# A two-layer convolution and GeGLU kernel: convolution steps borrow a PSUM bank only when the plan has it empty, and the last row's second half gets a bank of its own

## The chip, the cores and the metric

The kernel runs on one core of a Trainium2 chip, as one program with one launch. The metric is the device time of that core in microseconds; smaller is better. Every figure below is a time of a run, a row of its profile, or worked out from such rows.

## The reference, cut to what matters

Two kinds of layer alternate, twice. The first multiplies the normalised input by a long convolution (as long as the sequence, 2048 rows of 576 columns) of `shift(k) * v`; the second is a gated feed-forward block with 4608 hidden columns. Both are added to the residual.

```python
def _A_ref(q, k, v, shift_k, ssm_k, ssm_D):
    kv = k_shift * v                     # k_shift: four-tap causal filter of k
    y = irfft(rfft(kv, 2*S) * rfft(ssm_k, 2*S))[:S] + kv * ssm_D
    return q * y
def _B_ref(x, w_gate, w_up, w_down):
    return (_gelu(x @ w_gate) * (x @ w_up)) @ w_down
x = A_q
x = x + _A_ref(_layernorm(x), ...); x = x + _B_ref(_layernorm(x), ...)
x = x + _A_ref(_layernorm(x), ...); x = x + _B_ref(_layernorm(x), ...)
```

The convolution does not depend on `x`, so it is computed once and used by both layers.

## The kernel before, in words

**Units, passes, visits.** The 2048 rows are four chunks of 512 rows. A unit is one layer's feed-forward block on one chunk; there are eight units (0 to 7), in the order layer 0 of chunks 0 and 1, layer 1 of chunks 0 and 1, and the same for chunks 2 and 3. The units are done in passes of one or two (0; 1, 2; 3, 4; 5, 6; 7), and each pass goes three times over a third of the hidden columns. That makes 24 visits, numbered 0 to 23 here. One visit is:

- twelve pairs `gu` (matmuls of line 889, 216 records in all): gate and up for 128 hidden columns; ScalarE applies the gelu (line 1412, or 1403 and 1404) and VectorE multiplies (line 1413 or 1405) into `hT`;
- four rows `dn` (line 1428): each row is 24 matmuls, 12 hidden tiles by two halves of 288 columns, accumulated in one PSUM tile. When a row is done VectorE adds it to the residual `x_c`, which is called the eviction here (lines 1449, 1462, 1468 or 1470, by visit).

**Convolution.** It is a transform in blocks. A forward step is four matmuls of 288 columns (line 288, tile `cps`; "F" below). ScalarE copies its result out of PSUM into `eo` (line 291, two buffers), and VectorE makes a sum and a difference of the two halves (line 296, two instructions, the crossing). An inverse step is eight matmuls (line 331, "INV"), copied out by ScalarE or VectorE. Products in between are VectorE's (lines 304 to 321, 482). Chunk 0's convolution is done before visit 0; those of the other chunks are worked into the visits.

**PSUM.** It is cut into four tiles of two 512-element fp32 banks each; the code calls each such tile a bank, and so does this text. Three of them go round among `gu` pairs, `dn` rows and borrowed convolution steps: `pr(name)` counts `taken` up and gives the next in turn. The fourth is the convolution's own.

**The planner.** One Python pass writes every engine's instructions in order, with a model clock `t` (`t.pe`, `t.dve`, `t.act`) and a cost for each kind of instruction. The order is then fixed: each engine runs its instructions in that order, and waits at semaphores where a tile is not ready. Between two hidden tiles of a row, `fill` puts in what the clock says is ready: late evictions (`run_late`), VectorE work of the convolution (`run_v`), and TensorE steps of the convolution (`run_p`, line 568 on).

`run_p` takes the own bank if `ps_free[0]` says that it is free, and otherwise borrows: it needs `ps_free[1]`, the time at which the last borrowed step was copied out, to be past, and `conv.alt` to be set. `conv.alt` is set once for each row (line 1423) and used up by one borrow, so that a row has one borrow at most. What the bank that comes next in turn still holds is not asked.

The eviction of a row is put into the queue `late` at the row's end with the number `taken[0]` (line 1473), and written into VectorE's order when the clock is 0.2 us past the row's end (`run_late`), or at the latest when `pr` is about to come round (line 633).

The last row of the last visit is done half by half (lines 1433 to 1440): twelve matmuls into half 0 of the row's tile, an add on VectorE (line 1438), a store, then twelve matmuls into half 1 of the same tile, an add and a store.

Of the kernel before, what the change touches and what calls it, by code (L numbers as in the profile page):

```python
# [27 lines left out]
NEVER = 1e9  # L28
# [7 lines left out]
C_TT, C_ST, C_BN, C_NORM, C_HT, C_GELU, C_EVA, C_EVD, C_YH = 0.76, 0.82, 0.47, 0.62, 0.69, 0.6, 0.66, 0.76, 0.8  # L36
# [7 lines left out]
class Pace:  # L44


    def __init__(self):
        self.pe = self.dve = self.act = 0.0
# [84 lines left out]
class Conv:  # L133
# [9 lines left out]
    def __init__(self, tc, ctx, pace, A_k, A_v, A_shift_k, A_ssm_k, A_ssm_D, ident, cps, ypool):  # L143
        self.tc, self.nc, self.t = tc, tc.nc, pace
        self.k2, self.v2, self.hk = A_k[0], A_v[0], A_ssm_k
        self.S, self.D = self.k2.shape
        self.NB = self.S // BS
        self.KS = A_shift_k.shape[1]
        self.sk, self.sD = A_shift_k, A_ssm_D
        self.ident, self.cps, self.ypool = ident, cps, ypool  # L150
        D = self.D
        pool = lambda name, bufs: ctx.enter_context(tc.tile_pool(name=name, bufs=bufs))
        self.cst = pool("c_cst", 1)
        self.krp = pool("c_kr", 3)
# [12 lines left out]
        self.V_ = self.cst.tile([P, 2, RT, P], BF16, name="V")  # L167
        self.nV = self.cst.tile([P, 3, P], BF16, name="nV")
        self.skc = self.cst.tile([P, self.KS, D], BF16, name="skc")
        self.y, self.yb = {}, {}  # L170
        self.kt_, self.vt_ = {}, {}
        self.y_at = {(0, j): 0.0 for j in range(RT)}
        self.z_at = {0: 0.0}
        self.kv_at, self.fwd_at, self.hf_at, self.hd_at = {}, {}, {}, {}
        self.ht = {}
        self.y_used = {}
        self.ps_free, self.cur, self.alt = [0.0, 0.0], 0, None
        self.neo = 0
        self.U = deque()
        self.kr_free, self.hr_free = [0.0] * 3, [0.0] * 4  # L180
        self.nkr = self.nhr = 0
        self.V, self.L, self.Pq = deque(), deque(), deque()
        self.left = 0
        self.spills = deque()
# [383 lines left out]
    def run_p(self):  # L568
        t = self.t
        if not self.Pq:  # L570
            return False
        ready, cost, run = self.Pq[0]
        self.cur = 0 if self.ps_free[0] <= t.pe else 1
        if ready() > t.pe or self.ps_free[self.cur] > t.pe or self.cur and self.alt is None:
            return False
        self.Pq.popleft()
        run()
        t.pe += cost
        return True

@with_exitstack
def ssm_geglu_kernel(ctx, tc, A_q, A_k, A_v, A_shift_k, A_ssm_k, A_ssm_D, B_x, B_w_gate, B_w_up,
# [23 lines left out]
    t = Pace()  # L606
# [10 lines left out]
    turn, taken = list(range(4)), [0]  # L617

    def bank(n, name, shape=(P, 2, 512), dt=F32):
        return banks[n].tile(list(shape), dt, tag="pr", name=name)  # L620

    late = deque()

    def run_late(limit):
        if not late or late[0][0] > t.pe or max(t.dve, t.pe - 1.0) + C_EVD > limit:
            return False
        ready, _, run = late.popleft()
        run()
        t.on_dve(C_EVD, ready)
        return True  # L630

    def pr(name):
        while late and taken[0] - late[0][1] >= 2:
            ready, _, run = late.popleft()
            run()
            t.on_dve(C_EVD, ready)
        taken[0] += 1
        return bank(turn[(taken[0] - 1) % 3], name)
    ypool = pool("y", 2)
    xpool = pool("x", 2)  # L640
# [9 lines left out]
    conv = Conv(tc, ctx, t, A_k, A_v, A_shift_k, A_ssm_k, A_ssm_D, ident,  # L650
                lambda *form: bank(turn[3], "cps", *form), ypool)
# [183 lines left out]
    def out_tile():  # L835
        if not xn_open():
            spreads(True)
            conv.flush(NEVER)
        return xn_tile()
# [52 lines left out]
    def gu_half(pair, fi, n):  # L892
        gu(pair, wgu[fi // FG], fi % FG, lambda a: a.rearrange("p (j q) -> p j q", q=P)[:, n::2, :], xnT_of[0])
# [3 lines left out]
    def turn_row(ui, j, xn, when, entry):  # L897
# [17 lines left out]
        conv.ps_free[0] = xn_at[ui]  # L915
        xn_done[ui] = j + 1

    early = {}
    due = []

    def when_due(when, load, n):
        due.append((when, len(due), load, n))
        due.sort(key=lambda d: d[0])
# [44 lines left out]
    with tc.manual_schedule():  # L968
# [385 lines left out]
        for at, (wb, ph, ui, first, final) in enumerate(visits):  # L1354
# [30 lines left out]
            free, gone = deque([0.0] * 3), deque([0.0] * 2, maxlen=2)  # L1385
            conv.alt = None
            for fi in range(FP):
                n, gi = divmod(wb * FP + fi, FG)
                w = wgu[n]
                if wb == 0 and fi in early:  # L1390
                    pair = early.pop(fi)
                    taken[0] += 1
                    gu_half(pair, fi, 1)
                    t.pe = max(t.pe, free.popleft()) + C_GU / 2
                else:
                    pair = pr("gu")
                    gu(pair, w, gi, lambda a: a, xnT)
                    t.pe = max(t.pe, free.popleft()) + C_GU
                while run_late(NEVER):
                    pass  # L1400
                if hurry() and t.act <= t.pe + 0.2:
                    ga = work.tile([P, 2, CH], BF16, tag="ga", name="ga")
                    nc.scalar.activation(out=ga[:, 0, :], in_=pair[:, 0, :], func=ACT.Gelu_apprx_tanh)  # L1403
                    nc.scalar.copy(out=ga[:, 1, :], in_=pair[:, 1, :])  # L1404
                    nc.vector.tensor_tensor(out=hT[:, fi, :], in0=ga[:, 0, :], in1=ga[:, 1, :], op=ALU.mult)  # L1405
                    there = t.on_act(2 * C_GELU, max(t.pe + 0.15, gone[0]))
                    gone.append(t.on_dve(C_HB, there + 0.15) + 0.1)
                    free.append(there + 0.1)
                    lead = FAR
                else:  # L1410
                    ga = work.tile([P, CH], F32, tag="ga", name="ga")
                    nc.scalar.activation(out=ga[:], in_=pair[:, 0, :], func=ACT.Gelu_apprx_tanh)  # L1412
                    nc.vector.tensor_tensor(out=hT[:, fi, :], in0=ga[:], in1=pair[:, 1, :], op=ALU.mult)  # L1413
                    gone.append(t.on_dve(C_HT, t.on_act(C_GELU, max(t.pe + 0.15, gone[0])) + 0.15) + 0.1)
                    free.append(gone[-1])
                    lead = LEAD
                if gi == FG - 1 and final:
                    when_due(t.pe + (FP - FG) * C_GU + 12.0, load_wgu, n + 3)
                fill(t.pe + C_GU + lead, hurry(), conv.left > 0)
            ahead[:] = [t.pe + RT * FP * C_DN, visits[at + 1][2] if at + 1 < len(visits) else None]  # L1420
            for j in range(RT):
                acc = pr("dn")
                conv.alt = lambda: pr("cps")
                xa = x_c[c][:, j, :]
                xh = xa.rearrange("p (h d) -> p h d", h=2)

                def down(fi, h):
                    nc.tensor.matmul(acc[:, h, 0:HW], lhsT=hT[:, fi, j * P:(j + 1) * P],  # L1428
                                     rhs=wd[2 * wb + fi // WT][:, fi % WT, h * HW:(h + 1) * HW],
                                     start=(fi == 0), stop=(fi == FP - 1))  # L1430
                if wb == NWB - 1 and j == RT - 1:
                    dst = out2[c * CH:(c + 1) * CH, :].rearrange("(p j) d -> p j d", j=RT)[:, j, :]
                    for h in range(2):
                        for fi in range(FP):
                            down(fi, h)
                        ob, entry = out_tile()
                        entry[0] = True
                        nc.vector.tensor_tensor(out=ob[:, 0:HW], in0=xh[:, h, :], in1=acc[:, h, 0:HW], op=ALU.add)  # L1438
                        nc.sync.dma_start(out=dst[:, h * HW:(h + 1) * HW], in_=ob[:, 0:HW])
                    break  # L1440
# [6 lines left out]
                if layer == 1 and end:  # L1447
# [6 lines left out]
                        entry[0] = True  # L1454
                    else:
                        conv.store(dst, ob, t.pe + 0.2 + C_EVD + LAG, entry)
                    t.on_dve(C_EVD, t.pe + 0.2)
                else:
                    def plus(c=c, j=j, layer=layer, ph=ph, end=end, acc=acc, xa=xa, xh=xh):
                        if end:  # L1460
# [64 lines left out]
```

## Time and profile before

| | |
|---|---|
| runs of the kernel before | 947.65, 948.48, 947.70 us; median 947.70 |
| profiled execution | 947.87 us, of which the span from first to last instruction is 946.1 us |
| granted TensorE clock | 0.999 |
| busy share of the span | TensorE 98%, VectorE 58%, ScalarE 35%, GpSimd 15% |

Each row of the profile's timeline gives the start, the duration, the engine, the line, the operation with its tiles, and how many instructions were merged; a bracket at the end gives the idle time of the engine just before, and whose signal ended it. Matmuls overlap their successors, so the bracket is a little shorter than the delay: the delay is the distance of two starts less what back-to-back matmuls need. The records of `dn`, F and INV start 0.122 to 0.123 us apart when nothing waits.

### The profile page before, as it was taken

How to read it: one execution, taken by the hardware profiler on the slowest of the kernel's cores; microseconds unless marked ns; L12 is line 12 of the kernel's file. 1: busy time of each engine (PE TensorE's matmuls, PEld its weight loads, DVE VectorE, ACT ScalarE, POOL GpSimd, SP SyncE). 2: the span in 40 equal slices, each digit the busy share in tenths (PEclk: the TensorE clock that was granted, in tenths of full speed). 3: DMA queues.
4: the chain of work that ended last, by engine and by line, in shares of the span. 5: the costliest groups of instructions: out<-in, count | busy, mean ns of one | idle time of the engine just before them, and what ended most of it. 6: DMA issues, size and time to landing. Idle time of an engine off the chain costs nothing.

```text
span 946.1 us, 19330 instructions
## 1 busy us (share of the span) xinstructions
PE 930.2 (98%) x8225; PEld 539.2 (57%) x8225; DVE 552.5 (58%) x1033; ACT 327.5 (35%) x591; POOL 137.5 (15%) x302
## 2 busy tenths in 40 slices
PE   8999999999999999999999999999999999999998
PEld 5756465564655646556556556456456456456555
DVE  7767676577989856767988533543333334433322
ACT  5665426542324235441222511551211214411211
POOL 3213101331114005221110200130000002100000
PEclk9999999999999999999999999999999999999999
DMA  9997999348825603963770730592540540696620
GB/s 241 270 239 194 262 239 179 114 109 200 242 66 168 143 24 100 231 184 88 174 240 15 139 88 20 96 202 38 113 114 1 117 110 8 122 223 151 146 68 26
DMA packets 125324, 130.14 MB, mean 138 GB/s; under 512 B 39731, under 2 KB 117428, under 8 KB 125237
## 3 DMA queue, kind: packets, MB, share of 16 engines
q1 hardware_dynamic: 115906, 92.46, 45.5%
q0 software_dynamic: 9200, 35.54, 11.9%
q8 instruction: 64, 1.05, 0.5%
q10 hardware_dynamic: 130, 0.90, 0.3%
q14 instruction: 24, 0.19, 0.1%
HBM read 108.53 MB, written 11.80 MB: 127 GB/s over the span
## 4 chain that ended last, share of the span: by engine, by line
PE 96%; DVE 2%; DMA 1%; ACT 1%; issue 0%; POOL 0%; SPq 0%; ACTq 0%; DVEq 0%
PE gu L889 59%; PE dn L1428 29%; PE cps L288 2%; PE ps L279 2%; PE cps L331 1%; PE ps L889 1%; DMA k<-in_A_k_dram 1%; PE ps L1092 1%; PE ps L1198 1%; PE ps L1124 0%; PE ps L1219 0%; DVE x_c L1468 0%; DMA xnT<-xn 0%; DVE kc L296 0%; DVE x_c L1462 0%
## 5 line engine op out<-in xcount | busy, mean ns | idle before, releaser
L889 PE MATMUL gu<-xnT,wgu 64*128 64x512 bf16 x5130 | 559.0, 377 | 0.6 <-DMA xnT<-xn 0.6
L889 PEld LDWEIGHTS <-wgu 64*128 64x128 bf16 x5238 | 254.9, 94 | 304.7 <-issue 8.5
L1412 ACT ACTIVATE ga<-gu 128x512 f32<-128x512 f32 x256 | 152.8, 597 | 473.7 <-PE gu L889 468.3
L1413 DVE TENSOR_TENSOR hT<-ga,gu 128x512 bf16<-128x512 f32 x256 | 175.9, 687 | 230.2 <-ACT ga L1412 229.0
L1428 PE MATMUL dn<-wd,hT 128*128 128x288 bf16 x2304 | 294.3, 286 | 0.5 <-DVE xn L1438 0.5
L1428 PEld LDWEIGHTS <-hT 128*128 128x128 bf16 x2304 | 223.4, 98 | 66.1 <-issue 10.1
L1470 DVE TENSOR_TENSOR x_c<-x_c,dn 128x576 f32<-128x576 f32 x32 | 24.1, 753 | 41.4 <-PE dn L1428 41.1
L721 POOL TENSOR_SCALAR means<-s 128x1 f32<-128x1 f32 x28 | 11.3, 403 | 211.1 <-DVE x_c L1462 164.6
L291 ACT ACTIVATE eo<-cps 128x576 f32<-128x576 f32 x48 | 30.9, 651 | 27.1 <-PE cps L288 13.7
L1468 DVE SCALAR_TENSOR_TENSOR x_c<-dn,means,x_c 128x576 f32<-128x576 f32 x28 | 22.9, 817 | 27.8 <-PE dn L1428 27.5
L737 POOL TENSOR_TENSOR rstd<-ve,neghalf_t 128x1 f32<-128x1 f32 x56 | 34.4, 615 | 4.7
L308 DVE TENSOR_TENSOR prod<-prod 128x576 bf16<-128x576 bf16 x72 | 33.0, 458 | 2.5
L1403 ACT ACTIVATE ga<-gu 128x512 bf16<-128x512 f32 x29 | 17.3, 597 | 43.9 <-PE gu L889 40.7
L397 POOL DMA_DIRECT2D kr<-Kd x24 | 13.2, 551 | 102.6 <-DVE prod L307 102.6
L401 POOL DMA_DIRECT2D hr<-Hd x36 | 19.5, 541 | 45.4 <-DVE prod L307 45.4
L1449 DVE TENSOR_TENSOR xn<-x_c,dn 128x576 bf16<-128x576 f32 x15 | 11.3, 755 | 23.8 <-PE dn L1428 23.8
L1405 DVE TENSOR_TENSOR hT<-ga 128x512 bf16<-128x512 bf16 x31 | 13.1, 422 | 19.2 <-ACT ga L1404 19.2
L729 ACT ACTIVATE junk<-x_c,nm 128x576 bf16<-128x576 f32 x28 | 21.5, 767 | 5.6 <-POOL nm L721 5.6
L721 POOL TENSOR_SCALAR nm<-s 128x1 f32<-128x1 f32 x28 | 7.9, 281 | 100.3 <-DVE x_c L773 100.3
L763 ACT ACTIVATE yh<-y,rstd 128x576 f32<-128x576 bf16 x28 | 21.4, 769 | 2.7 <-POOL rstd L737 2.7
L296 DVE TENSOR_TENSOR kc<-eo 128x288 bf16<-128x288 f32 x48 | 19.4, 454 | 2.5 <-ACT eo L291 2.1
L736 POOL TENSOR_SCALAR ve<-ss 128x1 f32<-128x1 f32 x56 | 14.9, 266 | 39.3 <-ACT junk L729 39.2
(149 smaller groups left out, 601.4 us busy)
## 6 DMA issues: line engine op xcount, KB each, us to landing
wgu<-in_B_w_gate_dram SPq DMA_DIRECT2D x45, 576.0 KB, 5.6
wd<-in_B_w_down_dram SPq DMA_DIRECT2D x30, 864.0 KB, 8.2
wgu<-in_B_w_up_dram SPq DMA_DIRECT2D x45, 512.0 KB, 7.7
hr<-Hd POOLq DMA_DIRECT2D x36, 288.0 KB, 6.8
kr<-Kd POOLq DMA_DIRECT2D x24, 288.0 KB, 5.2
Kd<-kc POOLq DMA_DIRECT2D x12, 288.0 KB, 3.5
Hd<-hh POOLq DMA_DIRECT2D x12, 288.0 KB, 4.9
k<-in_A_k_dram POOLq DMA_DIRECT2D x3, 1008.0 KB, 11.8
```

What stands on the lines that cost most here:

```text
L291: nc.scalar.activation(out=eo[:], in_=ps[:, :, 0:HW], func=ACT.Copy, scale=scale)
L308: nc.vector.tensor_tensor(out=dst, in0=pr[:, 0, :], in1=pr[:, 1, :], op=ALU.subtract if part == 0 else ALU.add)
L401: nc.gpsimd.dma_start(out=hr[(kt, a)][1][:].rearrange("p s d -> p (s d)"), in_=self.Hd[m - a][kt])
L729: nc.scalar.activation(out=junk[:], in_=get_x(), func=ACT.Square, bias=v["nm"][:, 0:1], accum_out=v["ss"][:])
L737: nc.gpsimd.tensor_tensor(out=v["rstd"][:], in0=ve[:], in1=neghalf_t[:, 0:1], op=ALU.pow)
L763: nc.scalar.activation(out=g["yh"][:], in_=conv.y[c][:, j, :], func=ACT.Identity, scale=g["rstd"][:, 0:1], bias=1.0)
L889: nc.tensor.matmul(cols(pair[:, s, :]), lhsT=w[r0:r0 + HK, k, gi * P:(gi + 1) * P], rhs=cols(xnT[r0:r0 + HK, blk_of[k], :]), start=(k == 0 ...
L1412: nc.scalar.activation(out=ga[:], in_=pair[:, 0, :], func=ACT.Gelu_apprx_tanh)
L1413: nc.vector.tensor_tensor(out=hT[:, fi, :], in0=ga[:], in1=pair[:, 1, :], op=ALU.mult)
L1428: nc.tensor.matmul(acc[:, h, 0:HW], lhsT=hT[:, fi, j * P:(j + 1) * P], rhs=wd[2 * wb + fi // WT][:, fi % WT, h * HW:(h + 1) * HW], start=( ...
L1468: nc.vector.scalar_tensor_tensor(out=xh, in0=acc[:, :, 0:HW], scalar=m_[:, 0:1], in1=xh, op0=op, op1=ALU.add)
L1470: nc.vector.tensor_tensor(out=xh, in0=xh, in1=acc[:, :, 0:HW], op=ALU.add)
```

## The change

`run_p` now borrows only if `alt_at()` is past too. `alt_at` reads `bank_at`, a new list of three times, one for each bank that goes round. `pr` sets the entry of the bank it gives to "never"; the planner then writes the planned time of the bank's last read there: the gelu or the product for a `gu` pair, the eviction plus 0.15 us for a row. A borrowed bank is marked empty at once (`other`), since `ps_free[1]` stands for it. The entry of a late eviction is found by the number that goes with it in `late`.

In the last row, the second half takes a new tile from `pr`.

```diff
-        if ready() > t.pe or self.ps_free[self.cur] > t.pe or self.cur and self.alt is None:
+        if ready() > t.pe or self.ps_free[self.cur] > t.pe or self.cur and (self.alt is None or self.alt_at() > t.pe):
             return False
...
+    def other():
+        b = pr("cps")
+        bank_at[taken[0] % 3] = 0.0
+        return b
+
     def run_late(limit):
         if not late or late[0][0] > t.pe or max(t.dve, t.pe - 1.0) + C_EVD > limit:
             return False
-        ready, _, run = late.popleft()
+        add_late()
+        return True
+
+    def add_late():
+        ready, n, run = late.popleft()
         run()
-        t.on_dve(C_EVD, ready)
-        return True
+        bank_at[n % 3] = t.on_dve(C_EVD, ready) + 0.15
+
+    bank_at = [0.0] * 3
 
     def pr(name):
         while late and taken[0] - late[0][1] >= 2:
-            ready, _, run = late.popleft()
-            run()
-            t.on_dve(C_EVD, ready)
+            add_late()
         taken[0] += 1
+        bank_at[taken[0] % 3] = NEVER
         return bank(turn[(taken[0] - 1) % 3], name)
...
+    conv.alt_at = lambda: bank_at[(taken[0] + 1) % 3]
...
                     free.append(there + 0.1)
+                    bank_at[taken[0] % 3] = free[-1]
...
                     free.append(gone[-1])
+                    bank_at[taken[0] % 3] = free[-1]
...
                 acc = pr("dn")
-                conv.alt = lambda: pr("cps")
+                conv.alt = other
...
                     for h in range(2):
+                        if h:
+                            acc = pr("dn")
                         for fi in range(FP):
-                            down(fi, h)
+                            down(fi, h, acc)
...
-                    t.on_dve(C_EVD, t.pe + 0.2)
+                    bank_at[taken[0] % 3] = t.on_dve(C_EVD, t.pe + 0.2) + 0.15
```

More of the change, by code (lines that the diff above doesn't have):

```diff
@@ L176, in __init__ @@
         self.y_used = {}
-        self.ps_free, self.cur, self.alt = [0.0, 0.0], 0, None
+        self.ps_free, self.cur, self.alt, self.alt_at = [0.0, 0.0], 0, None, None
         self.neo = 0
@@ L1422, in ssm_geglu_kernel, with down @@
                 acc = pr("dn")
-                conv.alt = lambda: pr("cps")
+                conv.alt = other
                 xa = x_c[c][:, j, :]
                 xh = xa.rearrange("p (h d) -> p h d", h=2)
-                def down(fi, h):
+                def down(fi, h, acc=acc):
                     nc.tensor.matmul(acc[:, h, 0:HW], lhsT=hT[:, fi, j * P:(j + 1) * P],
```

## The prediction

> **What bounds the kernel now.** I read the page of the whole run first, then TensorE's waits, then TensorE's timeline where it waits.
>
> ```profile
> span 946.1 us, 19330 instructions
> PE 930.2 (98%) x8225; PEld 539.2 (57%) x8225; DVE 552.5 (58%) x1033; ACT 327.5 (35%) x591; POOL 137.5 (15%) x302
> PEclk9999999999999999999999999999999999999999
> PE 96%; DVE 2%; DMA 1%; ACT 1%; issue 0%; POOL 0%; SPq 0%; ACTq 0%; DVEq 0%
> PE gu L889 59%; PE dn L1428 29%; PE cps L288 2%; PE ps L279 2%; PE cps L331 1%; PE ps L889 1%; DMA k<-in_A_k_dram 1%; PE ps L1092 1%; PE ps L1198 1%; PE ps L1124 0%; PE ps L1219 0%; DVE x_c L1468 0%; DMA xnT<-xn 0%; DVE kc L296 0%; DVE x_c L1462 0%
> ```
>
> TensorE is busy for 98% of the span, is 96% of the chain that ends last, and runs at the full granted clock in all 40 slices. The change keeps its 8225 matmuls, so it can gain only what TensorE waits, and lose only by new waits. After the start-up (about 60 us, which the change leaves alone) the waits of TensorE are few:
>
> ```profile
> PE cps L288 <- DVE x_c L1468: 2.0, 3, 0.7
> PE cps L288 <- ACT eo L291: 1.3, 3, 0.7
> PE cps L288 <- DVE x_c L1462: 0.7, 1, 0.7
> PE dn L1428 <- DVE xn L1438: 0.5, 1, 0.5
> ```
>
> (Columns: total us, times, longest.) The first and third row are what the change is about: a forward step F waits until VectorE has evicted a feed-forward row. The fourth is the last row's second half. The second is F waiting for the copy of an earlier F out of PSUM; the change does not name it, but it moves F steps.
>
> **The borrow that waits (removed).** All four cases, on TensorE's timeline; in the third, VectorE's row stands between:
>
> ```profile
> 82.19 0.90 PE L1428 MATMUL dn<-wd,hT 128*128 128x288 bf16 x6
> 83.75 0.65 PE L288 MATMUL cps<-v,T 128*128 128x288 bf16 x4 [0.66 <-DVE x_c L1468]
> ...
> 87.91 0.90 PE L1428 MATMUL dn<-wd,hT 128*128 128x288 bf16 x6
> 89.48 0.28 PE L288 MATMUL cps<-v,T 128*128 128x288 bf16 x1 [0.66 <-DVE x_c L1468]
> ...
> 206.27 0.66 PE L1428 MATMUL dn<-wd,hT 128*128 128x288 bf16 x4
> 206.72 0.82 DVE L1468 SCALAR_TENSOR_TENSOR x_c<-dn,means,x_c 128x576 f32<-128x576 f32 x1 [0.93 <-PE dn L1428]
> 207.59 0.28 PE L288 MATMUL cps<-ht,T 128*128 128x288 bf16 x1 [0.66 <-DVE x_c L1468]
> ...
> 356.90 0.65 PE L1428 MATMUL dn<-wd,hT 128*128 128x288 bf16 x4
> 358.24 0.28 PE L288 MATMUL cps<-ht,T 128*128 128x288 bf16 x1 [0.69 <-DVE x_c L1462]
> ```
>
> Six `dn` matmuls at 0.1225 us from 82.19 would let F start at 82.93; it starts at 83.75, 0.82 late. The other three, worked out alike: 89.48 − 88.65 = 0.83, 207.59 − 206.76 = 0.83, 358.24 − 357.39 = 0.85. Together 3.33 us. The third shows how it comes about: the row ends two matmuls before F, its eviction starts at 206.72 and takes 0.82, and F borrows that very bank. It happens in the second row after a borrow: row A takes bank 1 and lends bank 2, row B takes bank 3, and the next bank in turn is bank 1, which row A has just left.
>
> In the order of the changed kernel's instructions (built, not run) all four borrows are gone. The `dn` matmuls and F steps of the five visits concerned, with F2 for two steps in a row:
>
> ```
> visit 0 before  2 F 6 F 12 F 6 F 2 F 8 F 8 F 6 F 2 F 44
>         after   2 F 6 F 12 F 8 F 8 F 8 F 6 F 2 F 8 F 36
> visit 3 before  26 F 2 F 2 F 8 F 8 F 4 F 2 F 44
>         after   26 F 2 F 2 F 8 F 8 F 8 F 8 F 34
> visit 4 before  2 F2 14 F 10 F 2 F 2 F 8 F 8 F 50
>         after   2 F2 14 F 10 F 8 F 8 F 8 F 2 F 44
> visit 7 before  2 F2 4 F 8 F 8 F 4 F 2 F 8 F 60
>         after   2 INV2 2 INV 10 INV 12 F 8 F 8 F 8 F 2 F 2 F 14 F 8 F 20
> visit 8 before  2 F2 8 F 8 F 8 F2 8 F 8 F 54
>         after   26 F2 8 F 8 F 8 F 8 F 8 F 8 F 22
> ```
>
> A row is 24 matmuls, so the four borrows stand at matmul 26 or 50, two into a row. The borrows that remain take banks whose last eviction lies a whole row back. The plan frees a row's bank 0.2 + 0.76 + 0.15 = 1.11 us after its last matmul; measured it is free after 207.59 − 206.76 = 0.83. So a borrow that the plan allows does not wait unless VectorE is more than 0.28 us behind the plan. Beyond its wording, the rule is stricter: after a borrow `taken[0]` is one ahead, so `late` carries the borrowed bank's number and the row's own bank stays at "never" until it is given out again. That forbids a borrow in the next row in any case, and so also the four above. I take the whole 3.33; the bounds are 0, if each is replaced by a wait for the own bank, and 3.33.
>
> **The last row's second half.**
>
> ```profile
> 930.14 10.46 PE L1428 MATMUL dn<-wd,hT 128*128 128x288 bf16 x84
> 940.64 0.46 DVE L1438 TENSOR_TENSOR xn<-x_c,dn 128x288 bf16<-128x288 f32 x1 [0.71 <-PE dn L1428]
> ...
> 941.14 1.63 PE L1428 MATMUL dn<-wd,hT 128*128 128x288 bf16 x12 [0.55 <-DVE xn L1438]
> ```
>
> 84 matmuls from 930.14 end their turn at 940.43; the second half starts at 941.14, 0.71 late, because it waits for the add that reads the first half's tile. The tile that the new `pr` gives was the second row's, evicted some 4 us before, so the wait goes. Nothing but the last add and its store follow, and the first half's store is issued earlier than the second's as before: 0.71 us, bounds 0.5 (the idle time in the bracket) and 0.71.
>
> **F steps moved to the own bank (added waits).** In before, 14 F steps follow the last one after exactly eight `dn` matmuls; in after, 21 do (counted in the table). Most of these use the own bank, which must be copied out in the meantime. How much room that leaves:
>
> ```profile
> 204.31 0.28 PE L288 MATMUL cps<-ht,T 128*128 128x288 bf16 x1 [0.66 <-ACT eo L291]
> 204.80 1.15 PE L1428 MATMUL dn<-wd,hT 128*128 128x288 bf16 x8
> 205.05 0.65 ACT L291 ACTIVATE eo<-cps 128x576 f32<-128x576 f32 x1 [0.79 <-PE cps L288]
> 205.78 0.29 PE L288 MATMUL cps<-ht,T 128*128 128x288 bf16 x1
> ```
>
> From F to F is 1.47 us; the copy ends 205.70 − 204.31 = 1.39 after F's start. So an own-bank step costs nothing if ScalarE starts the copy at once, with 0.08 to spare. ScalarE is late where `eo` has no free buffer (VectorE has not crossed the step before last) or other work stands before the copy. Those are the F steps that came late in before:
>
> ```profile
> 202.51 1.14 PE L1428 MATMUL dn<-wd,hT 128*128 128x288 bf16 x8
> 202.85 1.41 ACT L291 ACTIVATE eo<-cps 128x576 f32<-128x576 f32 x2 [0.96 <-DVE hh L296]
> ...
> 394.50 1.14 PE L1428 MATMUL dn<-wd,hT 128*128 128x288 bf16 x8
> 396.01 0.65 PE L288 MATMUL cps<-v,T 128*128 128x288 bf16 x4 [0.36 <-ACT eo L291]
> ...
> 400.19 1.14 PE L1428 MATMUL dn<-wd,hT 128*128 128x288 bf16 x8
> 401.64 0.28 PE L288 MATMUL cps<-v,T 128*128 128x288 bf16 x1 [0.30 <-ACT eo L291]
> ...
> 244.48 1.14 PE L1428 MATMUL dn<-wd,hT 128*128 128x288 bf16 x8
> 245.59 0.28 PE L288 MATMUL cps<-v,T 128*128 128x288 bf16 x1
> ```
>
> Late by 0.82 (204.31 against 203.49), 0.53, 0.47 and, the largest of the other eleven, 0.13. The big three follow two or three F steps close together (F 2 F 2 F in visit 3, F2 twice in visit 8); single file they come 0 to 0.13 late. After keeps the bunch in visit 3 with its 0.82, drops one of the two F2 in visit 8 (worth 0.47), and adds seven single steps: between 0 and 7 × 0.13 = 0.91. I take 0.47, the middle, so that this part comes to nothing; bounds −1.0 (visit 8's 0.53 goes too) and +0.91.
>
> **Visit 7.** Step 2's four INV move from the end of visit 6 into the start of visit 7; they are the same matmuls, and the same order INV2 2 INV 10 INV stands in visit 12 of before without a wait. What they delay: the F steps now share ScalarE with squares and gates of the next unit (lines 729 and 763). One square costs:
>
> ```profile
> 360.26 0.77 ACT L729 ACTIVATE junk<-x_c,means 128x576 bf16<-128x576 f32 x1
> ...
> 360.93 0.19 ACT L729 ACTIVATION_READ_ACCUMULATOR junk<-x_c,means 128x1 f32 x1
> ```
>
> Before a copy, 0.96 us of square can only partly hide: the copies leave 1.47 − 0.65 = 0.82 free in a period, so 0.14 shows. In the order of after, two squares and one gate stand between copies of own-bank steps: 0.3 us, bounds 0 and 0.82 (one full wait as in visit 3).
>
> The next unit's last row is normalised two `gu` pairs later in VectorE's order (after pair 11 of visit 8, not 9). On SP one group of gate and up weights is queued behind one more row's two transposes. Both are needed only when visit 9 starts:
>
> ```profile
> 389.81 3.80 SPq L844 DMA_TRANSPOSE xnT<-xn  x2
> ...
> 408.83 3.41 PE L889 MATMUL gu<-xnT,wgu 64*128 64x512 bf16 x30
> ```
>
> The last transposes end at 393.6, 15.2 us ahead. Two pairs are 3.9 us (a visit's twelve take 23.4, as the row at 174.15 under rival A) and a TensorE that is 4 us ahead takes another 4: over 7 us are left. Cost nothing; if that cover were gone, each us late would be a us.
>
> **Sum.** −3.33 − 0.71 + 0 + 0.3 = −3.74. The profiled execution took 947.87, which gives 944.13; it stands 0.17 above the median of the runs shown (947.70). So I forecast 944.0, and, most of the bounds of the terms taken in, 943 to 945.4 when the account is right.
>
> **The rivals.**
>
> A. The first two waits are only moved. Before visit 3 TensorE waits for data, and getting there 1.65 us earlier could just lengthen that:
>
> ```profile
> 162.25 0.76 DVE L1462 SCALAR_TENSOR_TENSOR x_c<-dn,x_c 128x576 f32<-128x576 f32 x1 [1.58 <-PE dn L1428]
> ...
> 174.15 23.27 PE L889 MATMUL gu<-xnT,wgu 64*128 64x512 bf16 x214 [0.60 <-DMA xnT<-xn]
> ```
>
> Against it: the chain that ends at 174.15 runs through VectorE, which at 162.25 had itself waited 1.58 for TensorE, so it moves along. For it: between the two lie ScalarE, GpSimd and DMA. If it holds: 944.0 + 1.65 = 945.6.
>
> B. The wait is exchanged for one on the own bank. A rule that speaks against the change is in the Trainium skill, Perfetto Trace Analysis, section Matmuls: independent groups should rotate through different banks so that the evacuation of one overlaps the next group's matmuls. The seven added steps reuse a bank that has just been written. If each showed its whole copy of 0.65 (the row at 205.05), that is 7 × 0.65 = 4.55 instead of 0.47: 948.1, no change. By that rule the trace agrees only in part: the `dn` matmuls between two F steps are in another bank and cover the copy, as 204.31 to 205.78 shows.
>
> C. Slower: VectorE doesn't keep up. A period of 1.47 holds a crossing (a step's two instructions of line 296), and in after the plan puts more products and filter steps of 0.75 between crossings. Then both `eo` buffers stay full, and every one of the 21 steps is as late as the bunched three, 0.6 on the mean: 12.6, where before had about 2.0. That gives 944.0 + 10.6 = 954.6. It decides (slower by over 1.9) once the 21 steps are late by some 0.37 each (7.7 us in all). VectorE's 58% speaks against it, its lateness in the three rows above for it.
>
> D. The change does not do what it says: the plan's "empty" is not the chip's. The borrows move, but wherever VectorE is behind the plan a borrow still meets a row being read. If all four remain at 0.83, only the tail counts: 944.0 + 3.33 = 947.3.
>
> **How the numbers follow.** A measurement of this kernel tells about 0.2% (1.9 us) from no change: faster is below 945.8. The account as summed gets 0.63, A 0.12, B and D together 0.14, C 0.07, and better than summed (more of the late F steps go) 0.04, at about 942.3. A and the upper part of the account lie about the bound, and give some of their chance to "same": faster 0.76, same 0.17, slower 0.07. The range is 942.6 to 946.8: from the better case to half way into B and D; the likeliest case's own is 943 to 945.4.
>
> **What the changed profile would show.** No wait of F on VectorE's evictions of `x_c` (it was 2.7 us in the waits). No wait of `dn` on line 1438's add (whatever its number then). F waiting for `eo` about as now, 1 to 2 us. The gap before visit 3 still 0.6; if it is 2, A holds. Visit 7 with one or two waits of 0.1 to 0.3. Wrong would make it: waits of F for `eo` over 5 us in all, a wait for `xnT` before visit 9, or VectorE waiting for a DMA in visits 7 and 8, which stops its queue, the crossings behind it, and so the copies and F.

## The result and the profile after

The changed kernel takes 943.18 us (median of 6 runs, 942.78 to 944.78); the kernel before took 947.82 beside it (median of 6). The ratio of the means is 0.9946, with a 95% interval of 0.9926 to 0.9966: faster by half a per cent, 0.8 us below the forecast of 944.0 and inside its range. The profiled execution is the one of 942.78. Of all executions in this text one was far slower, of the kernel before in the third batch below (1399.26 us at a granted clock of 0.66); it is in that batch's median and not in its ratios.

The page of the changed kernel: the span, the busy time of the engines, and the shares of the chain that ended last.

```profile
span 941.0 us, 19331 instructions
PE 928.4 (99%) x8225; PEld 538.7 (57%) x8225; DVE 550.2 (58%) x1033; ACT 327.0 (35%) x591; POOL 136.2 (14%) x302
PE 96%; DVE 1%; DMA 1%; ACT 1%; issue 0%; POOL 0%; SPq 0%; ACTq 0%; DVEq 0%
PE gu L898 59%; PE dn L1440 29%; PE cps L288 2%; PE ps L279 2%; PE cps L331 1%; DMA k<-in_A_k_dram 1%; PE ps L898 1%; PE ps L1208 1%; PE ps L1102 1%; PE ps L1134 0%; PE ps L1229 0%; DMA xnT<-xn 0%; DVE hh L296 0%; ACT eo L291 0%; PE ps L1305 0%
```

The 8225 matmuls are the same, and VectorE's evictions (`x_c`) are no longer among the chain's listed shares. TensorE's waits after the start-up (us in total, times, longest) are now two lines:

```profile
PE cps L288 <- ACT eo L291: 0.9, 2, 0.7
...
PE gu L898 <- DMA xnT<-xn: 0.6, 1, 0.6
```

The two kinds of wait that the change is about are gone: 2.7 us of F on evictions, and 0.5 of `dn` on the last row's add. On TensorE's timeline (start, duration, engine, line, operation, count), the second half of visit 0, the place of the former borrow in visit 7, and the end of the kernel:

```profile
81.80 1.14 PE L1440 MATMUL dn<-wd,hT 128*128 128x288 bf16 x8
82.78 0.65 PE L288 MATMUL cps<-v,T 128*128 128x288 bf16 x4
...
86.21 0.90 PE L1440 MATMUL dn<-wd,hT 128*128 128x288 bf16 x6
86.94 0.29 PE L288 MATMUL cps<-v,T 128*128 128x288 bf16 x1
...
88.17 1.14 PE L1440 MATMUL dn<-wd,hT 128*128 128x288 bf16 x8
89.27 0.28 PE L288 MATMUL cps<-v,T 128*128 128x288 bf16 x1
...
351.01 1.63 PE L1440 MATMUL dn<-wd,hT 128*128 128x288 bf16 x12
352.49 0.65 PE L288 MATMUL cps<-ht,T 128*128 128x288 bf16 x4
...
925.74 11.93 PE L1440 MATMUL dn<-wd,hT 128*128 128x288 bf16 x96
...
936.24 0.45 DVE L1452 TENSOR_TENSOR xn<-x_c,dn 128x288 bf16<-128x288 f32 x1 [0.72 <-PE dn L1440]
```

The four borrows stood two `dn` matmuls into a row. In visit 0 the first of them has become an F in the own bank, eight matmuls behind the F before it, and it is on time: 81.80 + 8 × 0.1225 = 82.78. The second, at matmul 50, still borrows (86.94; the bank of the F at 85.72 is not copied out by then), but a bank that no row of this visit has used, and it is on time too: 86.21 + 6 × 0.1225 = 86.95. In visit 7, F at matmul 26 is in the own bank, due at 351.01 + 12 × 0.1225 = 352.48 and not late. What is new is the last F of visit 0: due at 88.17 + 8 × 0.1225 = 89.15, it starts at 89.27, 0.12 late, behind a copy. The last 96 `dn` matmuls run in one piece, and the add at 936.24 lies beside them.

What is left of F's waits stands mostly in visit 3, which the change did not clear:

```profile
200.59 1.14 PE L1440 MATMUL dn<-wd,hT 128*128 128x288 bf16 x8
200.94 1.41 ACT L291 ACTIVATE eo<-cps 128x576 f32<-128x576 f32 x2 [0.96 <-DVE hh L296]
202.40 0.28 PE L288 MATMUL cps<-ht,T 128*128 128x288 bf16 x1 [0.66 <-ACT eo L291]
...
204.80 0.82 DVE L1482 SCALAR_TENSOR_TENSOR x_c<-dn,means,x_c 128x576 f32<-128x576 f32 x1 [0.93 <-PE dn L1440]
205.82 1.14 PE L1440 MATMUL dn<-wd,hT 128*128 128x288 bf16 x8
206.47 0.65 ACT L291 ACTIVATE eo<-cps 128x576 f32<-128x576 f32 x1 [1.22 <-DVE hh L296]
207.17 0.28 PE L288 MATMUL cps<-ht,T 128*128 128x288 bf16 x1 [0.20 <-ACT eo L291]
```

202.40 − (200.59 + 0.98) = 0.83 late, and 207.17 − 206.80 = 0.37. Both times the copy of the F before (ScalarE, line 291) had itself waited for VectorE's crossing (line 296), because both `eo` buffers were full. The second of the two, in the place of visit 3's former borrow, still goes back to an eviction: VectorE, which runs in order, stood 0.93 us until the row was done, evicted it from 204.80 on, and only then, at 205.53, came to the crossing. F no longer waits for the eviction itself, but for what stands behind it in VectorE's order.

To place the whole difference I took the distance of each two neighbouring matmul starts less what they need back to back, from the first `gu` matmul of visit 0 to the last matmul, in both traces:

| us | before | after | difference |
|---|---|---|---|
| F late on an eviction | 0.826 + 0.827 + 0.827 + 0.852 | 0 | −3.33 |
| last row's second half late | 0.708 | 0 | −0.71 |
| F late on a copy, visit 0 | 0 | 0.123 | +0.12 |
| visit 3 | 0.823 | 0.823 + 0.367 | +0.37 |
| visit 4 | 0.151 + 0.126 | 0.270 | −0.01 |
| visit 7 | 0.076 | 0 | −0.08 |
| visit 8 | 0.524 + 0.271 + 0.464 | 0.164 | −1.10 |
| gap before visit 3 | 0.760 | 0.763 | 0.00 |
| first `gu` after the span's start | 47.63 | 47.24 | −0.39 |

The sum, from unrounded values, is −5.12; the profiled executions differ by 947.87 − 942.78 = 5.09, the medians by 4.64. The last row is chance: the start-up is not touched, and over the profiled executions shown here the first `gu` starts between 46.85 and 48.00. The rows above it make −4.73. From the first `gu` to the last matmul it is 894.86 before and 890.15 after, −4.71; below, "path" is that time.

### The profile page after: what moved, and what is told of

It is laid out like the page before. It is cut to its first block, busy times and chain, and to the rows that moved or that the text cites. A ratio compares the mean times of both kernels' runs of the same rounds, so it can differ in the third digit from the quotient of the medians.

```text
span 941.0 us, 19331 instructions
## 1 busy us (share of the span) xinstructions
PE 928.4 (99%) x8225; PEld 538.7 (57%) x8225; DVE 550.2 (58%) x1033; ACT 327.0 (35%) x591; POOL 136.2 (14%) x302
## 4 chain that ended last, share of the span: by engine, by line
PE 96%; DVE 1%; DMA 1%; ACT 1%; issue 0%; POOL 0%; SPq 0%; ACTq 0%; DVEq 0%
PE gu L898 59%; PE dn L1440 29%; PE cps L288 2%; PE ps L279 2%; PE cps L331 1%; DMA k<-in_A_k_dram 1%; PE ps L898 1%; PE ps L1208 1%; PE ps L1102 1%; PE ps L1134 0%; PE ps L1229 0%; DMA xnT<-xn 0%; DVE hh L296 0%; ACT eo L291 0%; PE ps L1305 0%
## 5 line engine op out<-in xcount | busy, mean ns | idle before, releaser
L1476 DVE SCALAR_TENSOR_TENSOR x_c<-dn,x_c 128x576 f32<-128x576 f32 x16 | 12.1, 756 | 17.9 <-PE dn L1440 17.9
```

## The experiments

Three questions were open. Does the gain come from the two parts named, and does it add up? What keeps the borrows off the full banks: the plan's times, or the accident of numbering? And is F's own bank, which the change leans on, worse or better than a borrowed one? "In its batch" compares kernels that ran together on one chip; the kernel before took 948.60, 948.31 and 949.65 (medians) in the three batches. In the third, ten of its eleven runs spread from 947.84 to 954.98, so the ratios of that batch come out lower than those of the others for the same time; paths are the safer comparison between batches. The runs are called e1 to e4 (first batch), e7 to e10 (second) and e11 to e14 (third).

### The last row alone

```diff
 # before, last row
                     for h in range(2):
+                        if h:
+                            acc = pr("dn")
                         for fi in range(FP):
-                            down(fi, h)
+                            down(fi, h, acc)
```

> The kernel before with the second bank for the last row's second half alone. Theory (two separate gains): 0.7 us less than before, 947.1, the wait of the last dn matmuls on the add is gone, the four waits of F on the eviction of x_c (0.83 each) stay. Rival (the part is hidden behind the last stores): no change, 947.8.

Measured (e1): 947.37 us, ratio 0.9981 (0.9965 to 0.9998); path 894.20, so −0.66. TensorE's waits:

```profile
PE cps L288 <- DVE x_c L1470: 2.0, 3, 0.7
...
PE cps L288 <- DVE x_c L1464: 0.7, 1, 0.7
```

The waits on evictions are all there, that on the last row's add is gone. The second tile takes off the 0.71 and nothing else.

### The borrow rule alone

```diff
 # after, last row
                     for h in range(2):
-                        if h:
-                            acc = pr("dn")
```

> The changed kernel without the second bank at the end: the borrow rule alone. Theory: 3.33 us for the four waits on the eviction and 0.7 for fewer F steps waiting for the copy before, so 943.8, with the wait of 0.7 at the end back. Rival (the two parts are not independent, part of the gain is the scatter of the start-up): 945 to 946.

Measured (e2): 944.02 us, ratio 0.9949 (0.9928 to 0.9971); path 891.08, −3.78 against before. TensorE's waits, and the last row:

```profile
PE cps L288 <- ACT eo L291: 1.0, 3, 0.7
...
PE dn L1440 <- DVE xn L1450: 0.5, 1, 0.5
```

```profile
936.93 0.46 DVE L1450 TENSOR_TENSOR xn<-x_c,dn 128x288 bf16<-128x288 f32 x1 [0.71 <-PE dn L1440]
...
937.44 1.63 PE L1440 MATMUL dn<-wd,hT 128*128 128x288 bf16 x12 [0.55 <-DVE xn L1450]
```

The four waits on evictions are gone, the last row's is back. The two parts give −0.66 and −3.78, together −4.44, where the whole change gave −4.71; the 0.27 between is mostly F in visit 0, late by 0.33 here and 0.12 there with the same order of instructions.

### Numbers that are right

The prediction noted that after a borrow the row's time goes to the borrowed bank's entry, and the row's own bank stays at "never". This edit gives each row's time to the row's own entry.

```diff
                 acc = pr("dn")
+                row = taken[0]
...
-                    bank_at[taken[0] % 3] = t.on_dve(C_EVD, t.pe + 0.2) + 0.15
+                    bank_at[row % 3] = t.on_dve(C_EVD, t.pe + 0.2) + 0.15
...
-                    late.append((t.pe + 0.2, taken[0], plus))
+                    late.append((t.pe + 0.2, row, plus))
```

> The changed kernel with the row's own number kept for its eviction, so that the plan's time of the eviction really stands for the row's bank, also after a borrow. A borrow may then follow one row after another, 1.1 us after the row's end at the earliest instead of 0.25. Theory S (the plan's times are good enough): no F waits for an eviction, 943.2 within 0.8. Rival D (the plan's empty is not the chip's; the changed kernel is only saved by the accidental ban on a borrow in the next row): some of the four waits come back, 0.3 to 0.8 each, 944 to 946.

Measured (e3): 944.07 us, ratio 0.9969 (0.9946 to 0.9992); path 890.84, 0.69 above after's. One wait on an eviction is back. It stands in TensorE's waits, and in the timeline of visit 0 with VectorE's rows:

```profile
PE cps L288 <- DVE x_c L1483: 0.6, 1, 0.6
```

```profile
88.13 0.46 DVE L296 TENSOR_TENSOR kc<-eo 128x288 bf16<-128x288 f32 x1 [1.61 <-DMA Hd<-hh]
88.80 0.65 PE L1441 MATMUL dn<-wd,hT 128*128 128x288 bf16 x4
88.82 0.46 DVE L296 TENSOR_TENSOR kc<-eo 128x288 bf16<-128x288 f32 x1 [0.23 <-DMA Hd<-hh]
89.19 0.81 DVE L1483 SCALAR_TENSOR_TENSOR x_c<-dn,mv,x_c 128x576 f32<-128x576 f32 x1
90.06 0.28 PE L288 MATMUL cps<-v,T 128*128 128x288 bf16 x1 [0.61 <-DVE x_c L1483]
```

F was due at 88.80 + 4 × 0.1225 = 89.29 and starts at 90.06, 0.77 late: it borrowed a bank whose eviction ended at 90.00. The plan had that eviction done, but on the chip VectorE stood 1.61 us before the crossing ahead of it. The crossing writes into a buffer (`kc` and `hh` share four) that a DMA to `Hd` still read. So a bank that is empty in the plan is not always empty on the chip, which is rival D, at one of the borrows and not at four. (Whether it was the transfer that made VectorE late is taken up again below, with e11 and e14.)

That raises the question of what the plan's times do in the changed kernel. Built from the kernel before, a kernel that only forbids a borrow in the row after a borrow, and asks for no time of any bank, has the same instructions in the same order and with the same waits on every engine as the borrow rule alone (e2); with the second tile of the last row added, it has those of the changed kernel. It is the same program, so the times measured for e2 and for the changed kernel are its times. In this kernel, then, the list of times decides nothing: the whole of e2's gain comes from the ban that the numbering causes, and where the times do decide, in e3, one wait returns.

### No borrow in the rows at all

```diff
                 acc = pr("dn")
-                conv.alt = other
+                conv.alt = None
```

> The changed kernel with no borrowing at all in the dn rows: every F and every inverse step uses the convolution's own bank, eight or more dn matmuls apart. Theory (an own-bank step in single file is late by 0 to 0.13, only bunches cost more): TensorE's waits for the copy fall from 1.7 us to under 1, 942 to 943.5. Rival B (reusing the bank shows the copy): some ten more own-bank steps of up to 0.65 each, 946 to 950. Rival by delay (the convolution comes too late for a later visit): a wait for xnT before a visit, several us at one place.

Measured (e4): 942.33 us, ratio 0.9938 (0.9924 to 0.9952), below the borrow rule's 944.02 in its batch by more than the last row's 0.71; path 889.11, 1.04 below after's. All F steps of the visits are single file in one bank, and they wait 0.27 and 0.24 us in all of the kernel. ScalarE's copies in visit 3, the stretch where after is late by 0.83 and 0.37:

```profile
202.35 0.65 ACT L291 ACTIVATE eo<-cps 128x576 f32<-128x576 f32 x1 [0.82 <-PE cps L288]
203.82 0.65 ACT L291 ACTIVATE eo<-cps 128x576 f32<-128x576 f32 x1 [0.82 <-DVE kvt L262]
```

A copy every 1.47 us, 0.82 idle before each: F never catches up with the copies. Rival B, by which each such step shows its copy, falls: there are more of these steps here than in after, and less waiting. The rule of the Trainium skill, Perfetto Trace Analysis, section Matmuls, is that independent matmul groups should rotate through different banks so that the evacuation of one overlaps the next group's matmuls. In this stretch one bank for F meets its purpose: the `dn` matmuls between two F steps lie in other banks, and they cover the copy.

But not all of the 1.24 us saved on F waits (1.75 − 0.51) arrives. Before visit 3:

```profile
171.62 0.39 PE L898 MATMUL gu<-xnT,wgu 64*128 64x512 bf16 x2 [0.25 <-DMA xnT<-xn]
172.76 0.61 PE L898 MATMUL gu<-xnT,wgu 64*128 64x512 bf16 x4 [0.75 <-DMA xnT<-xn]
```

These are 0.31 and 0.91 late, 1.22 in place of 0.76. The second row comes 172.76 − 47.70 = 125.06 after the first `gu`; in after it was 172.24 − 47.24 = 125.00. TensorE gets there earlier and the data do not. (−1.24, +0.46 for the gap and −0.26 for two transposes at the end of visit 2 that come 0.13 late each in after and on time here make the −1.04.)

### Only inverse steps borrow

This asks whether F's borrows are what hurts, or borrows as such. F steps are kept to the own bank; inverse steps, which cost more than 0.9 us in the plan, may borrow.

```diff
-        if ... or self.cur and (self.alt is None or self.alt_at() > t.pe):
+        if ... or self.cur and (cost < 0.9 or self.alt is None or self.alt_at() > t.pe):
```

> The changed kernel with borrowing left to the inverse steps; F steps always use the own bank. Theory (without borrowing the gain is F in single file; the longer gap before visit 3, 1.2 against 0.76, came of the inverse steps spread over visit 2): F waits as without borrowing, under 0.6 in all, the gap back at 0.76, 941.9. Rival (the gap before visit 3 grows because TensorE comes earlier): as without borrowing, 942.3 or more.

Measured (e9): 941.98 us (940.88 to 942.14), ratio 0.9924 (0.9897 to 0.9951); the changed kernel, run again in this batch, took 943.27 (lowest 942.72). Path 888.90, 1.25 below after. After the start-up TensorE waits only here, before visit 3 (its timeline):

```profile
170.94 0.39 PE L898 MATMUL gu<-xnT,wgu 64*128 64x512 bf16 x2 [0.36 <-DVE xnT L919]
171.99 1.25 PE L898 MATMUL gu<-xnT,wgu 64*128 64x512 bf16 x10 [0.65 <-DMA xnT<-xn]
```

No F step waits. That takes 1.75 off; the gap before visit 3 takes 0.48 back (1.24, against 0.76), and the second `gu` group stands at 171.99 − 47.12 = 124.87 after the first `gu`. The forecast that inverse borrows would keep this gap at 0.76 was wrong: an F step of 0.49 that stood before it in after has moved into visit 3, and the data come only 0.13 earlier. That the time still came out at the 941.9 of the forecast is luck in part: F waits not at all, where the forecast left it up to 0.6.

This kernel computes what after does. Its median and its path are the lowest of the kernels with unchanged arithmetic, but e4, in another batch, is close (path 889.11) and the intervals of the two ratios overlap.

### The changed kernel again

No edit.

> The changed kernel as it is, for a comparison on the same chip with the three others: 943.2 by the first measurement, 942.8 to 944.2.

Measured (e10): 943.27 us, ratio 0.9949 (0.9927 to 0.9972); the same late steps (0.137, 0.822, 0.367, 0.270, 0.163), the first `gu` at 47.58 for 47.24, and a path of 890.16 for 890.15. The path repeats to 0.01 us while the start-up differs by 0.34.

### Faster crossings

The other reading of visit 3: F waits for the copy, the copy for a free `eo`, and that for VectorE's crossing. Here `eo` is bf16 instead of fp32, so that the two halves of a forward step are rounded once more before their sum and difference; the rest of the arithmetic is after's.

```diff
-        eo = self.eop.tile([P, 2, HW], F32, tag="eo", name="eo")
+        eo = self.eop.tile([P, 2, HW], BF16, tag="eo", name="eo")
```

> The changed kernel, same order, with eo kept in bf16 instead of fp32, still two buffers; the results of the forward steps are rounded once more. Only the crossings on VectorE may become shorter (0.41 us each now). Theory (the F steps that are still late wait for an eo buffer, which the crossing frees): the waits of F for the copy fall with the crossing's duration, by half at most, 942.3 to 943.2. Rival (the copy itself, or other work of ScalarE ahead of it, is what is late): no change, 943.2.

Measured (e7): 941.98 us, ratio 0.9931 (0.9909 to 0.9954). The profiled execution took 943.89, 2.6 us above the fastest of this kernel, and shows where. Visit 0, VectorE, ScalarE and TensorE:

```profile
89.68 0.31 DVE L296 TENSOR_TENSOR kc<-eo 128x288 bf16<-128x288 bf16 x1 [1.22 <-DMA Hd<-hh]
90.48 0.75 DVE L296 TENSOR_TENSOR kc<-eo 128x288 bf16<-128x288 bf16 x3 [0.49 <-DMA Hd<-hh]
90.91 0.65 ACT L291 ACTIVATE eo<-cps 128x576 bf16<-128x576 f32 x1 [1.82 <-DVE kc L296]
91.61 0.28 PE L288 MATMUL cps<-v,T 128*128 128x288 bf16 x1 [1.55 <-ACT eo L291]
```

One instruction of the crossing takes 0.31 us where it took 0.46, and in visit 3 F is late by 0.31 and 0.07 instead of 0.82 and 0.37. In visit 3 that is more than the half that was forecast at most, and the median lies below the forecast's 942.3 to 943.2. But in visit 0 VectorE is early enough to meet the transfer to `Hd`, waits 1.22 + 0.49 for it, and F is 1.71 late.

### Faster crossings and four buffers

```diff
-        self.eop = pool("c_eo", 2)
+        self.eop = pool("c_eo", 4)
...
-        eo = self.eop.tile([P, 2, HW], F32, tag="eo", name="eo")
+        eo = self.eop.tile([P, 2, HW], BF16, tag="eo", name="eo")
```

> As the kernel with bf16 eo, with four eo buffers in the space of the two. Theory (eo buffers): all five late F steps of the changed kernel (0.82, 0.37, 0.27, 0.16, 0.12) come on time, 1.7 us less, 941.5. Rival (ScalarE's other work): the waits stay at about 1.7, 943.2.

For comparison, the copies and one half of the crossings in after, a row for each (count, busy time, mean ns, idle time before and its releasers):

```profile
L291 ACT ACTIVATE eo<-cps 128x576 f32<-128x576 f32 x48 | 31.0, 651 | 30.9 <-PE cps L288 23.3 <-DVE kc L296 3.6 <-DVE hh L296 2.7
L296 DVE TENSOR_TENSOR kc<-eo 128x288 bf16<-128x288 f32 x48 | 19.2, 453 | 1.6 <-ACT eo L291 1.4
```

Measured (e8): 941.27 us (940.83 to 941.71), ratio 0.9917 (0.9886 to 0.9949); path 888.41, 1.74 below after, where F waited 1.75. The same rows here:

```profile
L291 ACT ACTIVATE eo<-cps 128x576 bf16<-128x576 f32 x48 | 31.0, 651 | 29.2 <-PE cps L288 26.5 <-DVE xn L1463 1.7 <-ACT junk L738 0.3
L296 DVE TENSOR_TENSOR kc<-eo 128x288 bf16<-128x288 bf16 x48 | 12.4, 303 | 4.3 <-ACT eo L291 3.7 <-DMA Hd<-hh 0.3
```

The copies wait for VectorE's crossings no more (in after 3.6 us for `kc` and 2.7 for `hh`), and no F is late: after the start-up TensorE waits for the data before visit 3 alone, 0.76 as before. So what was left of F's waits in after was the number of `eo` buffers and the pace of the crossings, not the bank: e8 has the order and the banks of after. Which of the two counts for more is not shown, as e8 changes both. The transfer to `Hd` still holds VectorE, for 0.3 us, and with two more buffers it reaches nobody.

### Both together

```diff
 # e9 (only inverse steps borrow), and
-        self.eop = pool("c_eo", 2)
+        self.eop = pool("c_eo", 4)
 # and eo in BF16
```

> F steps on the own bank only, inverse steps may borrow, and four bf16 eo buffers. Theory: nothing is left of F's waits in either single change, so both together give no more than one of them: 941.3 to 941.9. Rival (they add): 940.0 to 940.7.

Measured (e12): 941.76 us (941.25 to 941.93), ratio 0.9905 (0.9878 to 0.9932); path 888.91 against 888.90 of e9. Two cures for the same waits do not add up: once no F step waits, what is left is the gap before visit 3.

### The spill, three times

Three kernels ask whether the transfer to `Hd` is what returns a wait in e3 and spreads the executions of e7: one more buffer for `kc` and `hh` with after's borrows, the same with e3's numbers, and e3's numbers with the four buffers of before. All three have `eo` in bf16, in two buffers.

```diff
 # e13: after, e11: e3, both with
-N_KC = 4
+N_KC = 5
 # e14: e3, N_KC as before; all three with
-        eo = self.eop.tile([P, 2, HW], F32, tag="eo", name="eo")
+        eo = self.eop.tile([P, 2, HW], BF16, tag="eo", name="eo")
```

> The changed kernel with bf16 eo (two buffers) and, in the space that this frees, a fifth buffer for the crossed results (kc, hh). Theory (the long wait of F at 91.6 in the run with bf16 eo alone, and most of the scatter of its times, come of VectorE waiting in visit 0 until a spill of hh has left its buffer): VectorE no longer waits for a DMA there, no F step waits over 0.4 us, 941.4, and its runs lie within 1 us. Rival (the scatter comes from elsewhere): scatter of 2 to 4 us as with four buffers.

> The kernel with the row's own number for its eviction, with bf16 eo and the fifth kc buffer. Theory (the borrow that waited there for an eviction did so because VectorE stood at that spill): no F waits for an eviction, 941.5 to 942.2. Rival (the plan's times of VectorE are off in any case): a wait of 0.3 to 0.8 stays at the borrow near 90 us, 942.3 or more.

> The same without the fifth buffer: the row's own number and bf16 eo alone. Theory (the spill): the wait near 90 us is there again in the profiled run or in part of the runs, 942 to 943.5 with a larger scatter than with the fifth buffer. Rival (faster crossings alone cure it): as with the fifth buffer.

Measured (e13, e11, e14): e13 942.46 us (941.42 to 943.16), ratio 0.9912 (0.9885 to 0.9939); e11 943.21 (941.19 to 943.61), 0.992 (0.989 to 0.995); e14 942.48 (941.69 to 944.11), 0.9916 (0.9888 to 0.9943). VectorE's waits for the spill, over the whole kernel, first e11, then e14 (in e13 there is none):

```profile
DVE kc L296 <- DMA Hd<-hh: 1.6, 1, 1.6
```

```profile
DVE kc L296 <- DMA Hd<-hh: 2.2, 2, 1.9
```

In the traces the fifth buffer does what it should with after's borrows: e13's VectorE does not meet the transfer, and F is late only in visit 3 (0.31 and 0.07). With e3's numbers it is not enough: e11 still waits 1.6, though F is then only 0.23 late, where e14 with four buffers has 0.68. Both start right behind an eviction (88.25 after 88.20, and 88.75 after 88.70), so neither the forecast for e11 that no F waits for one nor its rival's 0.3 to 0.8 holds. The path of e7 less its late F is 890.49 − 1.71 = 888.78, and e13's is 888.79: in these two traces the transfer accounts for the difference.

The times do not follow. The six runs of e13 were forecast within 1 us and spread over 1.7, and its median is no lower than e7's 941.98 in another batch. e11 and e14 spread over 2.4 each, where the fifth buffer was to narrow it, and e11 has the higher median. So the transfer explains the late F in the executions whose traces show it, but not the spread of the times. What else makes it stays open: there is one trace of each kernel, and for these three it is of the fastest of the six executions.

## Why the prediction was right

**The borrow that waits.** Right in size and place: −3.33 was taken and −3.33 came. All four waits went, and e2 alone gives −3.78 with 0.48 of it from fewer waits on copies. The reason was right only as the prediction's aside had it. It named two: the plan frees a bank later (1.11 us) than it is measured free (0.83), and the numbering forbids a borrow in the next row anyhow. The second does the work alone. With the first alone, in e3, one wait of 0.77 returns: VectorE was there more than the 0.28 us behind the plan that the prediction gave as the bound.

**The last row's second half.** Right: −0.71, in after and alone in e1.

**F steps moved to the own bank.** Mis-sized. Taken as 0, from −0.47 for visit 8 and +0.47 for seven added steps; the trace has −0.69. Visit 8 gave −1.10, not −0.47: with the F2 that was dropped went 0.46 behind it and 0.27 within it, which the prediction had not counted, and the one that remains now makes a later F 0.16 late instead of 0.52. There less work of VectorE stood between the copies and their crossings: in before the crossings started 394.37 − 392.74 = 1.63 us after the copies, in after 393.65 − 392.38 = 1.27.

```profile
392.74 1.19 ACT L291 ACTIVATE eo<-cps 128x576 f32<-128x576 f32 x2 [0.24 <-PE cps L288]
...
394.37 2.44 DVE L296 TENSOR_TENSOR kc<-eo 128x288 bf16<-128x288 f32 x6
```

```profile
392.38 1.19 ACT L291 ACTIVATE eo<-cps 128x576 f32<-128x576 f32 x2 [3.18 <-PE cps L288]
...
393.65 2.44 DVE L296 TENSOR_TENSOR kc<-eo 128x288 bf16<-128x288 f32 x6
```

(The first fence is before, the second after.) The seven added steps cost 0.12 + 0.37 − 0.01 − 0.08 = 0.41, close to the 0.47 taken. The lower bound of −1.0 had named the other part, that "visit 8's 0.53 goes too": 0.36 of it went, and the uncounted 0.27 makes up for the rest.

**Visit 7.** Mis-sized: +0.3 was taken, and no F waits there. The prediction reckoned that 0.14 of a square must show, since 0.96 does not go into 0.82 of idle time. In after:

```profile
354.64 0.65 ACT L291 ACTIVATE eo<-cps 128x576 f32<-128x576 f32 x1 [0.82 <-PE cps L288]
355.19 0.77 ACT L738 ACTIVATE junk<-x_c,means 128x576 bf16<-128x576 f32 x1
355.86 0.19 ACT L738 ACTIVATION_READ_ACCUMULATOR junk<-x_c,means 128x1 f32 x1
356.16 0.65 ACT L291 ACTIVATE eo<-cps 128x576 f32<-128x576 f32 x1
```

These instructions on ScalarE overlap by about 0.1 us (the copy would end at 354.64 + 0.65 = 355.29, and the square starts at 355.19), so copy, square and read-out take 356.05 − 354.64 = 1.41 and not 0.65 + 0.96 = 1.61; a period of 1.47 holds them, and the copy at 356.16 follows its F, which starts at 355.43, by 0.73, where the copy without a square in the prediction's row at 205.05 follows by 0.74. Adding durations was the mistake; starts had to be subtracted. The covers named for the next unit's normalising and for SP's queue held: TensorE waits for no `xnT` before visit 9.

**The sum.** −3.74 forecast, −4.73 by the rows of the path: 0.69 and 0.3 are the two steps above. The profiled executions differ by 0.39 more through the start-up; the medians' −4.64 stands within 0.1 of the path.

**The rivals.** A fell for the change itself: the gap before visit 3 is 0.76 as before, though the group behind it starts 1.52 us sooner (125.00 after the first `gu`, for 174.15 − 47.63 = 126.52 in before): the data moved along. It came true for the next gain: in e4 and e9 TensorE comes earlier still and the gap takes 0.46 and 0.48 back. B fell, in e4 above all. C fell: F waits 1.75 in all, not 12.6, though VectorE's crossings are what those 1.75 wait for. D is shown by e3 at one borrow; the changed kernel escapes it by the ban, and not by the planned times that the title speaks of.

## What to carry to other kernels

A buffer that a plan calls empty is empty on the chip only as far as the engine that empties it keeps to the plan; a rule about order (not in the row after a borrow, or not at all for short steps) held here where one about planned times let a wait back in. Before a stage gets a second place for its results, look at whether the one that it has is covered: with 0.98 us of other matmuls between steps, one bank cost 0.51 us in all of e4 and nothing in e9, and borrowing bunched the steps until the next buffer down the line was full. When a change removes a wait, count also what the reordered steps no longer wait for, and compare paths from a fixed instruction, not spans.

## What the runs showed of the hardware

- TensorE's path of 890 us repeated to 0.01 us in two executions of the same kernel, while the start-up ahead of it moved by 0.34; over all profiled executions here the start-up moved by 1.15.
- A sum or difference of 288 columns took 453 ns from fp32 to bf16 and 303 ns from bf16 to bf16 on VectorE, a ratio of 1.5. The Trainium skill, VectorE: DVE Perf Modes, section "The perf-mode tier table (the rule you actually need)", has such an operation (`tensor_tensor`) at 2×, 1224 ns, for bf16 and at 1×, 2293 ns, for fp32, at 2048 columns. No run here has that size; at 288 columns the gain is smaller.
- The last row's two halves lie in two 512-element banks of one tile, and the matmuls into the second waited 0.71 us for an add that reads the first. With a tile each, the add at 936.24 lies beside the matmuls at no cost. The halves lie in different banks both times, so the wait came with the tile, not with the bank.
- A transfer out of a buffer held VectorE, and through it the copies and TensorE: 1.7 us in one execution of e7, in a stretch where in after nothing is late but one F by 0.12.
